# Transposing w3 on VectorE, from 32-row blocks, in place of TensorE

## Chip, core and metric

The kernel runs on one core of a Trainium2 chip. The metric is the device time of one execution in microseconds (us). The kernel before takes 873.46 us, the median of 3 runs (872.48 to 873.71). The profile shows one execution with a span of 870.7 us.

## What is computed

Eight batches of eight heads, 576 positions, 64 values per head. A retention (attention with a decay in place of a softmax) gives x, 4608 tokens by 512; a feed-forward block follows, in which two projections are multiplied element by element:

```python
scores = scale * np.matmul(q, k.transpose(0, 1, 3, 2))
ret = scores * Dmat[None, :, :, :]          # decay, zero above the diagonal
attn_out = np.matmul(ret, v)
x = attn_out.transpose(0, 2, 1, 3).reshape(B * S, H * D)   # 4608 x 512
a = x @ w1                                  # w1, w2: 512 x 1024
b = x @ w2
h = a * b @ w3                              # w3: 1024 x 1024
out = (h @ w_out).astype(np.float32)        # w_out: 1024 x 512
```

Queries, keys and values arrive as 32-bit floats; the four weights arrive as 64-bit floats, and the kernel converts them itself.

## The kernel before

The kernel doesn't compute h. It multiplies the two weights first, w3 @ w_out (1024 x 512, called w3o), once, and then a * b by w3o. This document is about that product of weights, a stage between the first feed-forward projections and the second half of the attention. TensorE takes its stationary operand transposed, so each block row of w3 (128 rows of 1024) has to be turned before it can be multiplied by w_out.

The weights are cut in blocks of 512 KB, 128 partitions by 512 numbers of 64 bits: 16 blocks for w1 and w2, 8 of w_out (`wo`), 16 of w3 (two for each block row). `load_block` fetches a block into one of five buffers:

```python
    blocks = []
    for fp in range(NQ):
        for j, w in enumerate((moe_w1, moe_w2)):
            for r in range(2):
                blocks.append((("w12", fp, j, r), w))
    blocks += [(("wo", g), moe_w_out) for g in range(KF)]
    blocks += [(("w3", ft, g0), moe_w3) for ft in range(KF) for g0 in range(0, DF, CV)]
    at = {key: n for n, (key, _) in enumerate(blocks)}
    loaded, begun, converted, turned = [0], [0], [0], [0]
...
    def load_block():
        n = loaded[0]
        if n == len(blocks):
            return
        key, w = blocks[n]
        t = raw.tile([P, CV, 2], I32, tag="raw", name="raw", bufs=5)
        if key[0] == "w12":
...
        else:
            r, c0 = (key[1], 0) if key[0] == "wo" else key[1:]
            nc.sync.dma_start(t, w[r * P:(r + 1) * P, c0:c0 + CV, :])
        live["raw", n] = t
        loaded[0] += 1
```

A block is converted by integer arithmetic on its two 32-bit halves: five instructions on VectorE and, between the third and the fourth, two on ScalarE. It is written as a generator, so that its steps can be laid between other work; `convert(n)` takes n steps.

```python
    def begin_block():
        n = begun[0]
        t = live["raw", n]
        lo, hi = t[:, :, 0], t[:, :, 1]
        e = raw.tile([P, CV], I32, tag="exp", name="e")
        m = raw.tile([P, CV], I32, tag="man", name="m")
        vec = nc.vector


        vec.tensor_scalar(out=e, in0=hi, scalar1=1, scalar2=21,
                          op0=ALU.logical_shift_left, op1=ALU.logical_shift_right)
        yield

        vec.tensor_scalar(out=m, in0=hi, scalar1=0x000FFFFF, scalar2=0x00100000,
                          op0=ALU.bitwise_and, op1=ALU.bitwise_or)
        yield
        vec.scalar_tensor_tensor(m.bitcast(F32), in0=lo.bitcast(U32), scalar=2.0 ** -32, in1=m,
                                 op0=ALU.mult, op1=ALU.add)
        relu = mybir.ActivationFunctionType.Relu
        nc.scalar.activation(e, e, relu, bias=lim[:, 0:1], scale=-1.0)
        nc.scalar.activation(e, e, relu, bias=lim[:, 1:2], scale=-2.0 ** 23)
        live["em", n] = e, m
        begun[0] += 1
        yield

    def end_block():
        n = converted[0]
        hi = live["raw", n][:, :, 1]
        e, m = live["em", n]
        vec = nc.vector
        vec.scalar_tensor_tensor(e, in0=hi, scalar=-(1 << 31), in1=e,
                                 op0=ALU.bitwise_and, op1=ALU.bitwise_or)
        yield
        key = blocks[n][0]
        while not (key[0] == "w12" or "wo" in live and (key[0] == "wo" or key[1] < turned[0] + 2)):
            yield "wait"
        out, m, e = converted_to(n), m.bitcast(F32), e.bitcast(F32)
        if key[0] == "w12":
            m, e = (x.rearrange("p (c n) -> p c n", c=2) for x in (m, e))
        vec.scalar_tensor_tensor(out, in0=m, scalar=2.0 ** -20, in1=e, op0=ALU.mult, op1=ALU.mult)
        converted[0] += 1

        if n >= 4:
            load_block()
        if key[0] == "w12" and key[1] > 0 and key[2:] == (1, 1):
            yield from strassen_weights(key[1])
        yield
```

In the conversion of a run of blocks, the beginning of the next block stands before the end of the present one:

```python
        yield from begin_block()
        while converted[0] < len(blocks):
            if begun[0] < len(blocks) and converted[0] not in (1, 2, 3):
                yield from begin_block()
            yield from end_block()
            if begun[0] == converted[0] < len(blocks):
                yield from begin_block()

```

The turning on TensorE and the product:

```python
    def w3_tr(ft):
        t = pools["wst"].tile([P, KF, P], F32, tag="w3T", name="w3T")
        for i in range(0, KF, NP):
            tp = acc.tile([P, NP, P], F32, tag="acc", name="tp")
            for n in range(NP):
                nc.tensor.transpose(tp[:, n, :], live["w3", ft][:, (i + n) * P:(i + n + 1) * P],
                                    ident)
            nc.scalar.copy(t[:, i:i + NP, :], tp)
        live["w3T", ft] = t

    def w3_mm(ft, part):
        if part == 0:
            live["w3ps"] = acc.tile([P, DM], F32, tag="acc", name="ps")
        ps = live["w3ps"]
        for g in range(part * NP, part * NP + NP):
            nc.tensor.matmul(ps, live["w3T", ft][:, g, :], live["wo"][:, g, :],
                             start=(g == 0), stop=(g == KF - 1))
        if part == 1:
            nc.scalar.copy(live["w3o"][:, ft, :], ps)
```

The up-projections (`up`) run on TensorE during the conversion; their additions on VectorE carry steps of the conversion between them:

```python
        def plus(ps, to, sb):
            nc.vector.tensor_add(c[:, to], ps, c[:, sb])
            convert(conv)
            if aside:
                aside.pop(0)()
...
        c = ffn.tile([P, 4, 2, TB], F32, tag="c", name="c", bufs=1)
        p1 = product(None, "A11", "B11")
        nc.scalar.copy(c[:, 0], p1)
        plus(product(None, "S2", "T2"), 1, 0)
        plus(product(None, "S3", "T3"), 2, 1)
        p5 = product(None, "S1", "T1")
        plus(p5, 3, 2)
        plus(product(None, "A22", "-T4"), 2, 2)
        product(p1, "A12", "B21")
        nc.scalar.copy(c[:, 0], p1)
        product(p5, "S4", "B22")
        plus(p5, 1, 1)
...
        nc.vector.tensor_mul(ab[:, 4 * fp:4 * fp + 4, :], c[:, :, 0, :], c[:, :, 1, :])
        if tail:
            convert(conv)
```

The loop of the stage. `todo` holds the up-projections left; when it is empty, the block rows follow each other:

```python
    live["wo"] = pools["wst"].tile([P, KF, DM], F32, tag="wo", name="wo", bufs=1)
    live["w3o"] = w3op.tile([P, KF, DM], F32, tag="w3o", name="w3o")
    todo = [(0, 1, 2), (0, 0, 3), (0, 1, 3)] + [(0, 2, fp) for fp in range(NQ - 1)]
    multiplied = 0
    while multiplied < KF:
        if todo:
            first = converted[0] < 4 * NQ
            up(*todo.pop(0), conv=2 if first else 1)
            convert(0 if first else 3)
        ft = multiplied
        begun_ft = ft < turned[0]
        if begun_ft:
            w3_mm(ft, 0)
        if turned[0] < KF and (not todo or converted[0] > at["w3", turned[0], DF - CV]):
            convert_up_to(at["w3", turned[0], DF - CV] + 1)
            w3_tr(turned[0])
            turned[0] += 1
        if begun_ft:
            w3_mm(ft, 1)
            multiplied += 1
        if not todo:
            convert(10)
    w3_part.close()
```

After it come the last up-projection of this token group, the down-projection by w3o, and the loads of the next heads (`ld_k`, `ld_q`, `ld_v`), which take the place in memory that the raw weight blocks had. Heads later in the kernel are already turned by VectorE (`front_blocks`, L198), from blocks of 32 rows, which the change now does for w3.

Of the kernel before, what the change touches and what calls it, by code (L numbers as in the profile page):

```python
# [8 lines left out]
F32 = mybir.dt.float32  # L9
I32 = mybir.dt.int32  # L10
U32 = mybir.dt.uint32
ALU = mybir.AluOpType
PSUM = bass.MemoryType.PSUM

# [22 lines left out]
def kernel(  # L39
# [13 lines left out]
    nc = tc.nc  # L53
    moe_w1, moe_w2, moe_w3, moe_w_out = (
        w.bitcast(I32).rearrange("r (c t) -> r c t", t=2) for w in (moe_w1, moe_w2, moe_w3, moe_w_out))
    B, H, S, D = q.shape
    DM = H * D
    DF = moe_w3.shape[0]
    CV = 512
    P = 128  # L60
    NP = H // 2
    NB2 = B // 2


    NC = (S + P - 1) // P
    short = S - (NC - 1) * P
    sizes = [short] + [P] * (NC - 1)
    starts = [0] + [short + c * P for c in range(NC - 1)]
    G = NB2 * NC
    NB = 3  # L70
    TB = S // NB
    NT = 2 * TB // P
    KD = DM // P
    KF = DF // P
# [13 lines left out]
    pools = {}  # L88
# [6 lines left out]
    open_attention(att_part)  # L95
    acc = ctx.enter_context(tc.tile_pool(name="acc", bufs=7, space=PSUM))
    st_ps = ctx.enter_context(tc.tile_pool(name="st_ps", bufs=1, space=PSUM))

    ctx.enter_context(tc.manual_schedule())

    live = {}
# [14 lines left out]
    ident = const.tile([P, P], F32, tag="ident", name="ident")  # L116
# [10 lines left out]
    gq = const.tile([P, NC, H], F32, tag="gq", name="gq")  # L127
    gqs = const.tile([P, NP, S // 32], F32, tag="gqs", name="gqs")
    dq = ffn.tile([P, 4, 2, TB], F32, tag="c", name="dq", bufs=1).rearrange("p a b s -> p (a b s)")[:H, :S]
# [6 lines left out]
    for c in (0, slice(1, NC)):  # L136
        n = short if c == 0 else P
# [16 lines left out]
    def strassen_weights(fp):  # L154
# [7 lines left out]
        tt("S4", "A12", "S2", ALU.subtract)  # L162
        live["S", fp] = True
        yield

    BL = 32

    def load_blocks(g, nm):

        i, c = divmod(g, NC)  # L170
        n = sizes[c] // BL
        t = pools["ld"].tile([P, 2 * NP, P // BL, BL], F32, tag="ld_q", name="bl_" + nm)
        src = {"k": k, "q": q}[nm][2 * i:2 * i + 2].rearrange("b (p a) s d -> a (b p) s d", a=2)
        for a in range(2):
            for f in range(D // BL):
                part = (a * (D // BL) + f) * BL
                for m in range(n):
                    s0 = starts[c] + m * BL
                    nc.sync.dma_start(t[part:part + BL, :, m, :],
                                      src[a, :, s0:s0 + BL, f * BL:(f + 1) * BL].rearrange("m r x -> r m x"))  # L180
        live["bl_" + nm, g] = t

    def scale_blocks(g):
# [3 lines left out]
        for b in range(2):  # L187
            part = t[:, b * NP:(b + 1) * NP, :n, :]
            nc.gpsimd.tensor_tensor(
                out=part, in0=part, in1=gqs[:, :, n0:n0 + n].unsqueeze(3).to_broadcast([P, NP, n, BL]),  # L190
                op=ALU.mult)

    def front_blocks(g):
        c = g % NC
        n = sizes[c] // BL
        for nm in "kq":
            dst = pools["fr"].tile([P, 2, NP, P], F32, tag=nm + "T", name=nm + "T", bufs=1 if nm == "k" else 2)
            nc.vector.transpose(  # L198
# [16 lines left out]
    def front(g, names="kq"):  # L215
        c = g % NC
        sz = sizes[c]
        for nm in names:
            src = live[nm, g]
            dst = pools["fr"].tile([P, 2, NP, P], F32, tag=nm + "T", name=nm + "T",  # L220
                                   bufs=1 if nm == "k" and g >= NC else 2)
# [87 lines left out]
    blocks = []  # L309
# [2 lines left out]
            for r in range(2):  # L312
                blocks.append((("w12", fp, j, r), w))
    blocks += [(("wo", g), moe_w_out) for g in range(KF)]
    blocks += [(("w3", ft, g0), moe_w3) for ft in range(KF) for g0 in range(0, DF, CV)]
    at = {key: n for n, (key, _) in enumerate(blocks)}
    loaded, begun, converted, turned = [0], [0], [0], [0]

    def load_block():
        n = loaded[0]  # L320
# [5 lines that stand above are left out]
            _, fp, _, r = key  # L326
            src = w[2 * r * P:2 * (r + 1) * P, fp * QC:(fp + 1) * QC, :]
            t2 = t.rearrange("p (c n) t -> p c n t", c=2)
            if r == 0:
                nc.sync.dma_start(t2, src.rearrange("(c p) n t -> p c n t", p=P))  # L330
            else:
                for half in range(2):
                    nc.sync.dma_start(t2[heads[half]],
                                      src.rearrange("(c a d) n t -> a d c n t", a=2, d=D)[1 - half])
        else:
            r, c0 = (key[1], 0) if key[0] == "wo" else key[1:]
            nc.sync.dma_start(t, w[r * P:(r + 1) * P, c0:c0 + CV, :])
        live["raw", n] = t
        loaded[0] += 1

    def converted_to(n):
        key, _ = blocks[n]
        if key[0] == "w12":
            _, fp, j, r = key
            return wA[fp // 2][:, j, 2 * r:2 * r + 2, fp % 2 * QC:fp % 2 * QC + QC]
        if key[0] == "wo":
            return live["wo"][:, key[1], :]
        _, ft, g0 = key
        if ("w3", ft) not in live:
            live["w3", ft] = pools["wst"].tile([P, DF], F32, tag="w3", name="w3")  # L350
        return live["w3", ft][:, g0:g0 + CV]

    def begin_block():
        n = begun[0]
# [23 lines left out]
# [6 lines that stand above are left out]
                                 op0=ALU.bitwise_and, op1=ALU.bitwise_or)  # L384
        yield
        key = blocks[n][0]
        while not (key[0] == "w12" or "wo" in live and (key[0] == "wo" or key[1] < turned[0] + 2)):
            yield "wait"
        out, m, e = converted_to(n), m.bitcast(F32), e.bitcast(F32)
        if key[0] == "w12":  # L390
            m, e = (x.rearrange("p (c n) -> p c n", c=2) for x in (m, e))
        vec.scalar_tensor_tensor(out, in0=m, scalar=2.0 ** -20, in1=e, op0=ALU.mult, op1=ALU.mult)  # L392
        converted[0] += 1

        if n >= 4:
# [4 lines that stand above are left out]
# [22 lines left out]
    def convert(n):  # L422

        for _ in range(n):
            if go_on() is not None:
                return

    def convert_up_to(n):
        while converted[0] < n:
            assert go_on() is None  # L430


    def w3_tr(ft):
        t = pools["wst"].tile([P, KF, P], F32, tag="w3T", name="w3T")
        for i in range(0, KF, NP):
            tp = acc.tile([P, NP, P], F32, tag="acc", name="tp")
            for n in range(NP):
                nc.tensor.transpose(tp[:, n, :], live["w3", ft][:, (i + n) * P:(i + n + 1) * P],  # L438
                                    ident)
            nc.scalar.copy(t[:, i:i + NP, :], tp)  # L440
        live["w3T", ft] = t

    def w3_mm(ft, part):
        if part == 0:
            live["w3ps"] = acc.tile([P, DM], F32, tag="acc", name="ps")
        ps = live["w3ps"]
        for g in range(part * NP, part * NP + NP):
            nc.tensor.matmul(ps, live["w3T", ft][:, g, :], live["wo"][:, g, :],  # L448
                             start=(g == 0), stop=(g == KF - 1))
        if part == 1:  # L450
            nc.scalar.copy(live["w3o"][:, ft, :], ps)

    every = [(i, n) for i in range(NB2) for n in range(NB)]

# [190 lines left out]


    load_block()
    load(0, "v")
    load_block()
    load(1, "kq")  # L650
    load_block()
# [65 lines left out]
    for a in range(2):  # L717
        for f in range(D // BL):
            part = (a * (D // BL) + f) * BL
# [6 lines left out]
    live["wo"] = pools["wst"].tile([P, KF, DM], F32, tag="wo", name="wo", bufs=1)  # L726
    live["w3o"] = w3op.tile([P, KF, DM], F32, tag="w3o", name="w3o")
    todo = [(0, 1, 2), (0, 0, 3), (0, 1, 3)] + [(0, 2, fp) for fp in range(NQ - 1)]
    multiplied = 0
    while multiplied < KF:  # L730
        if todo:
            first = converted[0] < 4 * NQ
            up(*todo.pop(0), conv=2 if first else 1)
            convert(0 if first else 3)
        ft = multiplied
        begun_ft = ft < turned[0]
        if begun_ft:
            w3_mm(ft, 0)
        if turned[0] < KF and (not todo or converted[0] > at["w3", turned[0], DF - CV]):
            convert_up_to(at["w3", turned[0], DF - CV] + 1)  # L740
            w3_tr(turned[0])
            turned[0] += 1
        if begun_ft:
            w3_mm(ft, 1)
            multiplied += 1
        if not todo:
            convert(10)
    w3_part.close()


# [15 lines left out]
    todo = [(down, (0, 0), (0, 1)), (down, (1, 0), (1, 1)), (down, (0, 2), (1, 2))]  # L766
# [38 lines left out]
    for g in range(NC, G):  # L805
        c = g % NC
        n = -(-len(todo) // (NC - c))
# [78 lines left out]
```

## Time and profile before

| what | value |
|---|---|
| time, median of 3 runs | 873.46 us |
| span of the profiled execution | 870.7 us |
| TensorE (PE) busy in it | 851.9 us |
| VectorE (DVE) busy | 458.3 us |
| ScalarE (ACT) busy | 194.7 us |
| GpSimd (POOL) busy | 111.8 us |
| first transpose of w3 on TensorE | 158.79 us from the start |
| first matmul after the stage | 222.57 us from the start |

How the lines are read: a group has its source line, engine, operation, the tile written and the tiles read, the shape and the count; after the first bar the busy time of all in us and the mean length of one in ns; after the second the time for which the engine stood idle just before them, with what ended most of it. "PEld" is the loading of TensorE's weights, beside its matmuls. The chain of waits is followed back from the last instruction: at each step to what released it, or to the instruction before it on its engine. In a timeline each row has its start and its length in us; a bracket at the end gives the idle time before it, and the releaser. "issue" is time in which an engine waited for nothing that the profile shows.

### The profile page before, as it was taken

The page shows a single profiled execution, that of the slowest core. Times are in us where ns is not written, and L with a number is a line of the kernel's source. Part 1 is how long each engine was busy: PE and PEld are TensorE (multiplying, and loading weights), DVE is VectorE, ACT ScalarE, POOL GpSimd, SP SyncE. Part 2 cuts the span into 40 slices and gives each one's busy share as a digit, 9 for nine tenths or more (in the row PEclk, how much of TensorE's full clock was granted, in tenths as well). Part 3 has the DMA queues.
Part 4 walks back from the last instruction along what each step waited for, and adds up shares of the span by engine and source line. Part 5 has one row for each costly group of instructions (what it writes and reads, how often), then busy time and mean ns, then how long its engine had stood idle before and what let it go on. Part 6 is the DMA issues. An engine that isn't in the chain of part 4 may idle for free.

```text
span 870.7 us, 15305 instructions
## 1 busy us (share of the span) xinstructions
PE 851.9 (98%) x6373; PEld 779.0 (89%) x6373; DVE 458.3 (53%) x781; ACT 194.7 (22%) x390; POOL 111.8 (13%) x91
## 2 busy tenths in 40 slices
PE   5899999999999999999999999999999999999998
PEld 5899999645888999999999999999999999999996
DVE  4799998973543344643544544534543434334343
ACT  3676333553022221101111101111101100001000
POOL 3000020002001323201212030230300101000000
PEclk9999999999999999999999999999999999999999
DMA  9993443437035444515242335061300000000001
GB/s 194 218 223 107 98 99 104 139 120 108 1 77 118 114 63 82 95 28 93 49 84 44 55 68 96 27 104 34 59 25 25 2 25 1 25 24 1 25 1 49
DMA packets 187332, 63.20 MB, mean 73 GB/s; under 512 B 175480, under 2 KB 175480, under 8 KB 187264
## 3 DMA queue, kind: packets, MB, share of 16 engines
q1 hardware_dynamic: 154624, 54.07, 29.2%
q10 hardware_dynamic: 32640, 8.16, 4.9%
q8 instruction: 50, 0.82, 0.4%
q14 instruction: 18, 0.15, 0.1%
HBM read 52.76 MB, written 9.44 MB: 71 GB/s over the span
## 4 chain that ended last, share of the span: by engine, by line
PE 88%; DVE 3%; issue 1%; DMA 1%; ACT 1%; DVEq 0%; ACTq 0%; SPq 0%
PE up L493 46%; PE po L599 25%; PE ps L448 6%; PE sc L241 4%; PE xps L298 3%; PE xps L291 2%; PE tp L226 1%; PE st L263 1%; DVE c L498 1%; PE tp L438 1%; DVE e L383 0%; DMA raw<-in_moe_w_dram 0%; ACT e L372 0%; DVE ab L519 0%; DVE w L392 0%
## 5 line engine op out<-in xcount | busy, mean ns | idle before, releaser
L498 DVE TENSOR_TENSOR c<-up,c 128x384 f32<-128x384 f32 x240 | 133.2, 555 | 198.0 <-PE up L493 193.2
L493 PE MATMUL up<-xT,wA 128*128 128x192 f32 x1152 | 213.5, 329 | 1.0 <-ACT xT L303 1.0
L493 PEld LDWEIGHTS up<-xT,wA 128*128 128x128 f32 x1152 | 191.9, 191 | 3.6 <-ACT xT L303 1.2
L493 PE MATMUL up<-T,wS 128*128 128x192 f32 x768 | 141.1, 327 | 2.1 <-DVE T L467 2.1
L493 PEld LDWEIGHTS up<-T,wS 128*128 128x128 f32 x768 | 127.8, 191 | 2.4 <-issue 2.4
L599 PE MATMUL po<-w3o,ab 128*128 128x256 f32 x456 | 104.2, 381 | 0.3 <-ACT ot L621 0.3
L599 PEld LDWEIGHTS po<-w3o,ab 128*128 128x128 f32 x456 | 86.0, 190 | 12.1 <-ACT ot L621 0.7
L603 DVE TENSOR_TENSOR ot<-po,ot 128x256 f32<-128x256 f32 x90 | 38.1, 424 | 72.3 <-PE po L599 70.6
L513 ACT COPY c<-up 128x384 f32<-128x384 f32 x48 | 22.9, 477 | 226.3 <-PE up L493 222.0
L493 PE MATMUL up<-xT,wS 128*128 128x192 f32 x384 | 70.6, 327 | 0.6 <-DVE c L498 0.5
L493 PE MATMUL up<-T,wA 128*128 128x192 f32 x384 | 70.3, 326 | 0.0
L244 DVE TENSOR_TENSOR pm<-sc,mask 128x512 f32<-128x512 f32 (+1 forms) x80 | 45.5, 628 | 46.7 <-PE sc L241 46.5
L599 PE MATMUL po<-wB,forms 128*128 128x256 f32 x288 | 65.1, 379 | 0.0
L493 PEld LDWEIGHTS up<-xT,wS 128*128 128x128 f32 x384 | 63.6, 190 | 1.5 <-DVE c L498 1.5
L493 PEld LDWEIGHTS up<-T,wA 128*128 128x128 f32 x384 | 63.7, 190 | 0.0
L599 PEld LDWEIGHTS po<-wB,forms 128*128 128x128 f32 x288 | 54.8, 190 | 7.3
L212 POOL TENSOR_TENSOR ld_v<-ld_v,gk 128x1024 f32<-128x1024 f32 (+1 forms) x17 | 32.3, 1900 | 213.6 <-DMA ld_v<-in_v_dram 186.3
L448 PE MATMUL ps<-wo,w3T 128*128 128x512 f32 x128 | 56.4, 593 | 0.2 <-ACT w3T L440 0.2
L506 ACT COPY c<-up 128x384 f32<-128x384 f32 x48 | 22.8, 476 | 117.4 <-PE up L493 68.4
L467 POOL TENSOR_TENSOR T<-xT,T 128x384 f32<-128x384 f32 x20 | 20.9, 1043 | 217.1 <-PE up L493 215.4
L519 DVE TENSOR_TENSOR ab<-c 128x768 f32<-128x768 f32 x48 | 46.6, 972 | 3.8
L448 PEld LDWEIGHTS ps<-wo,w3T 128*128 128x128 f32 x128 | 23.7, 190 | 27.2 <-issue 26.7
(75 smaller groups left out, 817.8 us busy)
## 6 DMA issues: line engine op xcount, KB each, us to landing
raw<-in_moe_w_dram SPq DMA_DIRECT2D x24, 512.0 KB, 3.7
out_dram<-ot SPq DMA_DIRECT2D x24, 256.0 KB, 2.0
bl_q<-in_q_dram SPq DMA_DIRECT2D x136, 32.0 KB, 2.1
bl_k<-in_k_dram SPq DMA_DIRECT2D x136, 32.0 KB, 2.2
raw<-in_moe_w_dram SPq DMA_DIRECT2D x16, 256.0 KB, 6.1
ld_k<-in_k_dram SPq DMA_DIRECT2D x8, 512.0 KB, 7.1
ld_q<-in_q_dram SPq DMA_DIRECT2D x8, 512.0 KB, 8.2
ld_v<-in_v_dram SPq DMA_DIRECT2D x8, 512.0 KB, 7.4
```

What stands on the lines that cost most here:

```text
L212: nc.gpsimd.tensor_tensor(out=t, in0=t, in1=gam[:sz, c].unsqueeze(1).unsqueeze(3).to_broadcast([sz, 2, H, D]), op=ALU.mult)
L241: nc.tensor.matmul(sc[j][:sz, p, :sz], kT[hs, b, p, :sz], qT[hs, b, p, :sz], start=True, stop=True)
L244: nc.vector.tensor_mul(pm[:sz, b, j, :, :sz], sc[j][:sz, :, :sz], mask[:sz, :sz].unsqueeze(1).to_broadcast([sz, NP, sz]))
L298: nc.tensor.matmul(banks[r][heads[half], b, n, :sz], vs[:sz, b * H + 2 * p + j, :], pm[:sz, b, j, p, :sz], start=(c == 0 and m == 0), stop ...
L448: nc.tensor.matmul(ps, live["w3T", ft][:, g, :], live["wo"][:, g, :], start=(g == 0), stop=(g == KF - 1))
L493: nc.tensor.matmul(ps[:, w, :], a[:, w, r, :], b[:, r, :], start=(new and w == r == 0), stop=(w == r == 1), skip_group_check=True)
L498: nc.vector.tensor_add(c[:, to], ps, c[:, sb])
L506: nc.scalar.copy(c[:, 0], p1)
L513: nc.scalar.copy(c[:, 0], p1)
L519: nc.vector.tensor_mul(ab[:, 4 * fp:4 * fp + 4, :], c[:, :, 0, :], c[:, :, 1, :])
L599: nc.tensor.matmul(ps[nm], a[A][:, f, :], live["W"][B][:, f, :], start=(f == 0 and not on), stop=(f == NP - 1), skip_group_check=True)
L603: nc.vector.tensor_add(ot[:, to[0], to[1]], ps[nm], ot[:, sb[0], sb[1]])
```

## The change

w3 is loaded in another layout and turned by VectorE in place of TensorE. VectorE's transpose turns each 32 x 32 square within its own 32 partitions. So the four quarters of a block row's columns are put on the four groups of 32 partitions, each with its rows in four blocks of 32; a transpose of 128 x 1024 then gives the whole block row turned, in SBUF, with the 1024 columns of w3 in another order on partitions. The rows of w_out are loaded in the same other order, so that the product is the same. What it is for: TensorE is left to multiply, and ScalarE need not copy turned blocks out of PSUM. The conversion's arithmetic stays as it was.

The diff, cut to its core (declarations moved, blank lines and the renaming of a counter left out):

```diff
 load_block:
-        else:
-            r, c0 = (key[1], 0) if key[0] == "wo" else key[1:]
-            nc.sync.dma_start(t, w[r * P:(r + 1) * P, c0:c0 + CV, :])
+        elif key[0] == "wo":
+            nc.sync.dma_start(t, w.rearrange("(a i x) n t -> i a x n t", i=KF, x=BL)[key[1]])
+        else:
+            _, ft, h = key
+            src = w[ft * P:(ft + 1) * P].rearrange("(j r) (a h f) t -> h a r j f t", r=BL, a=QP, h=DF // CV)
+            for a in range(QP):
+                nc.sync.dma_start(t[a * BL:(a + 1) * BL].rearrange("p (j f) t -> p j f t", j=P // BL), src[h, a])
 converted_to:
-        if ("w3", ft) not in live:
-            live["w3", ft] = pools["wst"].tile([P, DF], F32, tag="w3", name="w3")
-        return live["w3", ft][:, g0:g0 + CV]
+        if h == 0:
+            live["w3"] = pools["wst"].tile([P, P // BL, DF // CV, CV // QP], F32, tag="w3", name="w3", bufs=1)
+        return live["w3"][:, :, h, :]
 end_block:
-        while not (key[0] == "w12" or "wo" in live and (key[0] == "wo" or key[1] < turned[0] + 2)):
+        while not (key[0] == "w12" or "wo" in live and (key[0] == "wo" or key[1] < multiplied[0] + 3)):
             yield "wait"
         ...
         vec.scalar_tensor_tensor(out, in0=m, scalar=2.0 ** -20, in1=e, op0=ALU.mult, op1=ALU.mult)
+        if key[0] == "w3" and key[2] == DF // CV - 1:
+            yield
+            t = pools["wst"].tile([P, KF, P], F32, tag="w3T", name="w3T", bufs=3)
+            vec.transpose(t.rearrange("p i (j r) -> p j i r", r=BL),
+                          live["w3"].rearrange("p j h f -> p (j h f)"))
+            live["w3T", key[1]] = t
 the product:
-    def w3_tr(ft):
-        ...                                  # 8 transposes on TensorE, 2 copies on ScalarE
-    def w3_mm(ft, part):
-        ...                                  # half of the 8 matmuls at a time
+    def w3_mm(ft):
+        ps = acc.tile([P, DM], F32, tag="acc", name="ps")
+        for g in range(KF):
             nc.tensor.matmul(ps, live["w3T", ft][:, g, :], live["wo"][:, g, :],
                              start=(g == 0), stop=(g == KF - 1))
+        nc.scalar.copy(live["w3o"][:, ft, :], ps)
+        multiplied[0] += 1
 the loop:
+    while multiplied[0] < KF:
+        ft = multiplied[0]
+        done = at["w3", ft, DF // CV - 1] + 1
+        ready = converted[0] >= done
         if todo:
             first = converted[0] < 4 * NQ
             up(*todo.pop(0), conv=2 if first else 1)
             convert(0 if first else 3)
-        ...                                  # w3_mm half, w3_tr of the next, w3_mm half
+        if ready or not todo:
+            convert_up_to(done)
+            w3_mm(ft)
         if not todo:
-            convert(10)
+            convert(11)
```

In the program that results, the eight products stand in a row on TensorE, behind the same up-projection as the first transposes did before. On ScalarE the copy of each product (`w3o`) stands ahead of the activations of two blocks.

More of the change, by code (lines that the diff above doesn't have):

```diff
@@ L60 @@
     P = 128
+    BL = 32
+    QP = P // BL
     NP = H // 2
@@ L164, in strassen_weights @@
         yield
-    BL = 32
     def load_blocks(g, nm):
@@ L314 @@
     blocks += [(("wo", g), moe_w_out) for g in range(KF)]
-    blocks += [(("w3", ft, g0), moe_w3) for ft in range(KF) for g0 in range(0, DF, CV)]
+    blocks += [(("w3", ft, h), moe_w3) for ft in range(KF) for h in range(DF // CV)]
     at = {key: n for n, (key, _) in enumerate(blocks)}
-    loaded, begun, converted, turned = [0], [0], [0], [0]
+    loaded, begun, converted, multiplied = [0], [0], [0], [0]
     def load_block():
@@ L347, in converted_to @@
             return live["wo"][:, key[1], :]
-        _, ft, g0 = key
-        if ("w3", ft) not in live:
-            live["w3", ft] = pools["wst"].tile([P, DF], F32, tag="w3", name="w3")
-        return live["w3", ft][:, g0:g0 + CV]
+        _, ft, h = key
+        if h == 0:
+            live["w3"] = pools["wst"].tile([P, P // BL, DF // CV, CV // QP], F32, tag="w3", name="w3", bufs=1)
+        return live["w3"][:, :, h, :]
     def begin_block():
@@ L391, in end_block @@
             m, e = (x.rearrange("p (c n) -> p c n", c=2) for x in (m, e))
+        if key[0] == "w3":
+            m, e = (x.rearrange("p (c n) -> p c n", c=P // BL) for x in (m, e))
         vec.scalar_tensor_tensor(out, in0=m, scalar=2.0 ** -20, in1=e, op0=ALU.mult, op1=ALU.mult)
+        if key[0] == "w3" and key[2] == DF // CV - 1:
[4 more added lines that the diff above has]
+            live["w3T", key[1]] = t
         converted[0] += 1
@@ L430, in convert_up_to @@
             assert go_on() is None
-    def w3_tr(ft):
[L434 to L441, printed above, removed]
-    def w3_mm(ft, part):
[L444 to L447, printed above, removed]
+    def w3_mm(ft):
+        ps = acc.tile([P, DM], F32, tag="acc", name="ps")
+        for g in range(KF):
             nc.tensor.matmul(ps, live["w3T", ft][:, g, :], live["wo"][:, g, :],
                              start=(g == 0), stop=(g == KF - 1))
-        if part == 1:
-            nc.scalar.copy(live["w3o"][:, ft, :], ps)
+        nc.scalar.copy(live["w3o"][:, ft, :], ps)
+        multiplied[0] += 1
     every = [(i, n) for i in range(NB2) for n in range(NB)]
@@ L728 @@
     todo = [(0, 1, 2), (0, 0, 3), (0, 1, 3)] + [(0, 2, fp) for fp in range(NQ - 1)]
-    multiplied = 0
-    while multiplied < KF:
+    while multiplied[0] < KF:
+        ft = multiplied[0]
+        done = at["w3", ft, DF // CV - 1] + 1
+        ready = converted[0] >= done
         if todo:
@@ L734 @@
             convert(0 if first else 3)
[L735 to L745, printed above, removed]
+        if ready or not todo:
+            convert_up_to(done)
+            w3_mm(ft)
         if not todo:
-            convert(10)
+            convert(11)
     w3_part.close()
```

## The prediction

> **What bounds the kernel now.** I read the page first. Section 1 says which engine is full, section 2 whether it is full throughout and at what clock.
>
> ```profile
> PE 851.9 (98%) x6373; PEld 779.0 (89%) x6373; DVE 458.3 (53%) x781; ACT 194.7 (22%) x390; POOL 111.8 (13%) x91
> ...
> PEclk9999999999999999999999999999999999999999
> ```
>
> TensorE is busy 98% of the span at full clock, so a microsecond taken off TensorE is worth a microsecond unless another engine's wait takes its place. VectorE's 53% is an average over stages. The change touches only one stage, w3 @ w_out, so I look there next: the groups of instructions, shapes kept apart, for the lines of this stage (x128 stands for 64 matmuls of the program: an f32 matmul is recorded twice, a transpose once).
>
> ```profile
> L448 PE MATMUL ps<-wo,w3T 128*128 128x512 f32 x128 | 56.4, 593 | 0.2 <-ACT w3T L440 0.2
> L440 ACT COPY w3T<-tp 128x512 f32<-128x512 f32 x16 | 8.6, 587 | 5.9 <-PE tp L438 5.8
> L438 PE MATMUL tp<-ident,w 128*128 128x128 f32 x64 | 8.5, 273 | 1.1 <-DVE w L392 1.1
> L392 DVE SCALAR_TENSOR_TENSOR w<-m,e 128x512 f32<-128x512 f32 x16 | 11.1, 691 | 0.9
> L198 DVE STREAM_TRANSPOSE kT<-bl_k 128x1024 f32<-128x1024 f32 x8 | 9.9, 1239 | 0.0
> L198 DVE STREAM_TRANSPOSE qT<-bl_q 128x1024 f32<-128x1024 f32 x8 | 9.6, 1202 | 0.0
> ```
>
> 273 ns is the length of one transpose, not its price, since they overlap. The price comes from the chain of waits, in order of time, in this stage:
>
> ```profile
> 164.51 0.70 DVE w L392
> 165.21 0.14 issue
> 165.35 0.63 PE tp L438 x4
> 165.98 6.87 PE ps L448 x16
> 172.84 0.88 PE tp L438 x8
> 173.72 6.87 PE ps L448 x16
> ```
>
> From 165.35 on the chain stays on TensorE until the stage ends at 222.6 (the next stage's first matmul is there at 222.57). One block row of w3 costs 6.87 + 0.88 = 7.75 us: 8 matmuls at 0.86, 8 transposes at 0.11. VectorE keeps up with slack: the table by stage gives it 5.59 us of work in the 7.74 us from 180.43. Its timeline shows its waits, all on ScalarE:
>
> ```profile
> 184.35 0.69 DVE L369 SCALAR_TENSOR_TENSOR m<-raw,m 128x512 f32<-128x512 uint32 x1
> 186.92 0.69 DVE L383 SCALAR_TENSOR_TENSOR e<-raw,e 128x512 int32<-128x512 int32 x1 [1.88 <-ACT e L373]
> ```
>
> and ScalarE's timeline shows why: its queue is in order, and the copy of a finished product stands ahead of the two activations that VectorE waits for.
>
> ```profile
> 184.93 0.58 ACT L451 COPY w3o<-ps 128x512 f32<-128x512 f32 x1 [2.79 <-PE ps L448]
> 185.41 0.72 ACT L372 ACTIVATE e<-e,lim 128x512 int32<-128x512 int32 x1
> 186.17 0.72 ACT L373 ACTIVATE e<-e,lim 128x512 int32<-128x512 int32 x1
> ```
>
> So there is a loop TensorE, ScalarE, VectorE, TensorE already. It costs nothing now, because TensorE is always the last of it.
>
> [...]
>
> **The change part by part.**
>
> Removed, TensorE: 64 transposes, 8 x 0.88 = 7.0 us, all on the path, and the first wait for VectorE (1.14 us before 165.35) and for the first copy (0.24 at 160.07) in their present form. If nothing took their place, the stage would be 8 x 6.87 = 55.0 us from 158.8 to 213.8 in place of 222.6: at most 8.8 us, 1.0%, to be had.
>
> Removed, ScalarE: 16 copies of 587 ns, 1.07 us per block row. Off the path in steady state, but it shortens the loop.
>
> Added, VectorE: 8 transposes of 128x1024, 1.24 us each by the L198 rows (same size and type; only the output is written in blocks of 32 columns). They stand between w's second half and the next block's conversion.
>
> Moved: the loads of w3 become 64 DMAs of 128 KB in place of 16 of 512 KB. The DMA share in 168.5 to 188.4 is 0.46, five raw buffers run ahead, and VectorE's waits in this stage name no DMA. I count 0. The product is no longer cut in two around the next transposes: 8 matmuls in a row once the transposed block row is there. w3 has one buffer, w3T three, in place of two and two: the same room, and VectorE may still run ahead.
>
> Now the steady state, by engine and block row:
> - TensorE 6.87.
> - VectorE: the pitches of the timeline between starts (0.34, 0.45, 0.61, 0.76, 0.73 for the five conversions of one block) make 2.89, twice is 5.78, plus the transpose, 1.24 less the 0.08 by which such instructions overlap: about 7.0. So VectorE is now slightly slower than TensorE.
> - The loop. In the order of the changed program on ScalarE, each w3o copy stands ahead of two pairs of activations; the first pair belongs to the block row two further on. From the start of product k: 6.87 to its end, 0.04 + 0.48 for the copy, 1.51 for the pair, then on VectorE e 0.80, w 0.73, the begin of the next block 1.40, e 0.72, w 0.73, transpose 1.24, 0.05 to the start of product k+2. The sum is 14.57 for two block rows, 7.28 each. This is the longest of the three.
>
> The start: the first transpose falls into the last up-product, after the addition at 156.78, so it runs about 157.3 to 158.5, ready when TensorE has finished the up-product at 158.8: product 0 runs 158.8 to 165.7. VectorE's w of the next block row ended at 165.2 (164.51 + 0.70); one transpose ahead of it delays it by 1.16 and its own transpose ends at 167.6. So product 1 starts at 167.7, a wait of 2.0 us. From there: product 2 at 174.6 (VectorE), 3 at 182.3 (loop: 167.7 + 14.57), 4 at 189.3, 5 at 196.8, 6 at 203.9. For the last one no block is left to begin, which takes 1.40 off the loop: 196.8 + 13.2 = 210.0, but product 6 ends at 210.8, so product 7 runs 210.8 to 217.7. The stage ends 222.6 - 217.7 = **4.9 us** earlier, of the 8.8 at most. The rest is 2.0 at the start and some 1.9 in small waits of 0.1 to 0.8 us.
>
> After the stage: VectorE's last conversion ends about 4 us later than now (208.4 against 204.5 + 0.7), so the loads of the next heads, which wait for its buffers and start at 203.1 now, move to about 206.5. Their last scaling on GpSimd ends at 219.6 now, so at about 223; TensorE wants these heads at 243.9 - 4.9 = 239.0. Hidden by 16 us. The gain stays.
>
> Sum: 873.5 - 4.9 = **868.6 us**, 0.6% less.
>
> **The rivals.**
> - VectorE becomes the bound by more than I count. For it: 7.0 against 6.87 leaves no slack, and the transpose writes its output scattered in pieces of 128 B, which L198 doesn't quite do. [...] Each 0.1 us more on a transpose is 0.8 us in all; at 2 us a transpose the gain is gone (about 874), at 4 us it is some 890.
> - The loop doesn't bind, because the activations come sooner or waits overlap. Then 7.0 per block row, one microsecond or so better: 867.5. The floor, TensorE alone, is 873.5 - 8.8 = 864.7, only if the start had no wait either.
> - The loads become the bound: four issues per block on one queue, smaller pieces. For it: each piece is a quarter as long. Against: a block is needed every 3.5 us, one issue takes 0.33 us now, so four take about 1.3, and the DMA engines are half idle. If it did bind at 5 us a block, the stage would take 80 us, about 890.
> - The transposes were hidden anyway. Against: the chain lists them, each 0.88 us, in every block row. Then the time would stay at 873.
>
> **Range and chances.** The step I can misjudge is the wait per block row: 0.3 us either way on seven rows is about 2 us, and a slower transpose pulls only up. So 866.8 to 871.5 for 8 in 10. The ceiling of 1.0% rules out faster by over 2%; slower by over 2% (891) needs a transpose of 4 us or loads at 5 us a block.
>
> **What would show it.** Right: the 64 TensorE transposes and L440's copies gone; 8 VectorE transposes 128x1024 near 1.24 us; the product's matmuls still 64 at 6.87 us per eight; one wait near 2 us before product 1, then starts 6.9 to 7.7 us apart; the chain of waits in this stage alternating between TensorE, ScalarE's w3o copy and activations, and VectorE; the first matmul after it near 217.7; no DMA named in VectorE's waits. Wrong: transposes of 2 us or more, VectorE waiting for raw, or TensorE waiting for keys and queries near 240 us.

## The result, and the profile after

The changed kernel takes 877.02 us (median of 4 runs, 875.72 to 877.11); the kernel before, on the same chip, 873.10 (4 runs). The ratio is 1.0041, with a 95% interval of 1.0024 to 1.0059: the change costs 3.9 us where I had expected a gain of 4.9. The profiled spans are 875.0 and 870.7 us.

The page of the changed kernel, sections 1 and 2:

```profile
PE 848.9 (97%) x6309; PEld 773.9 (88%) x6309; DVE 469.8 (54%) x789; ACT 186.0 (21%) x374; POOL 113.5 (13%) x91
PEclk9999998999999999999999999999999999999999
```

The transposes are off TensorE: 64 instructions fewer than before. Yet it is busy only 3.0 us less (851.9 before), though 7.0 us of work were taken off. The one 8 in the row of its clock says where to look: the seventh slice is 131 to 153 us, ahead of the stage that the change is about.

The groups of the stage itself, shapes kept apart:

```profile
L450 PE MATMUL ps<-wo,w3T 128*128 128x512 f32 x128 | 56.1, 596 | 2.9 <-DVE w3T L404 2.9
L404 DVE STREAM_TRANSPOSE w3T<-w 128x1024 f32<-128x1024 f32 x8 | 9.9, 1244 | 0.6
```

The product is the same work as before (56.1 us against 56.4), its waits come to 2.9 us in all, and a transpose by VectorE takes 1244 ns. TensorE's timeline shows the stage from its first product to the first matmul of the next stage (start, length, and in brackets the idle time before it with its releaser):

```profile
166.37 7.03 PE L450 MATMUL ps<-wo,w3T 128*128 128x512 f32 x16
174.72 13.97 PE L450 MATMUL ps<-wo,w3T 128*128 128x512 f32 x32 [1.32 <-DVE w3T L404]
189.53 14.10 PE L450 MATMUL ps<-wo,w3T 128*128 128x512 f32 x32 [0.84 <-DVE w3T L404]
204.37 20.97 PE L450 MATMUL ps<-wo,w3T 128*128 128x512 f32 x48 [0.74 <-DVE w3T L404]
225.17 1.46 PE L495 MATMUL up<-xT,wA 128*128 128x192 f32 x8
```

From 166.37 to 225.17 are 58.80 us. Before, the same stretch (first transpose at 158.79 to 222.57) was 63.78. **The stage is 4.98 us shorter, as predicted (4.9), but it begins 7.6 us later.** The loss lies before it. Going back in the same timeline, I found the place:

```profile
129.69 1.46 PE L495 MATMUL up<-xT,wA 128*128 128x192 f32 x8
134.63 2.93 PE L495 MATMUL up<-xT,wS 128*128 128x192 f32 x8 [3.48 <-DVE c L500]
137.35 2.77 PE L495 MATMUL up<-xT,wA 128*128 128x192 f32 x8
139.91 1.67 PE L495 MATMUL up<-T,wS 128*128 128x192 f32 x8
```

TensorE stands idle for 3.48 us, waiting for an addition by VectorE, and then two groups of 8 matmuls take 2.93 and 2.77 us in place of 1.46. VectorE's timeline says why it was late, and the table by stage (stretch, its length, busy time of TensorE, its weight loads, VectorE, ScalarE and GpSimd, then granted clock, share of the DMA engines, GB/s) what the matmuls ran at:

```profile
131.81 0.43 DVE L368 TENSOR_SCALAR e<-raw 128x512 int32<-128x512 int32 x1 [4.41 <-DMA raw<-in_moe_w_out_dram]
```

```profile
134.60:138.00 3.40, 3.37 (x11) 3.37 (x12) 2.04 (x4) 0.00 (x0) 0.00 (x0) 0.50 0.45 147
```

VectorE waited for a block of **w_out**, which the prediction never looked at. Set against the profile of a repaired version (e1 below), the same instruction is later in the changed kernel by 1.1 us at 67 us, by 4.75 where TensorE resumes after the idle time (129.9 against 134.6), by 7.43 when the two slow groups are done (132.5 against 139.9), and by 8.4 at the end. So the parts of the loss are 1.1 in the first 67 us, 3.6 of idle time, 2.7 of half clock and 0.95 after it. Of this last, 0.74 is one wait of TensorE for ScalarE near the end (1.04 us at 862.47, 0.30 in e1); e2 below, with w_out loaded in the same way, has 0.31 there, so this part isn't w_out's.

Why was the block late? The diff also reorders the loading of w_out: its rows must stand in the order in which the new transpose leaves the columns of w3. In the stretch from 95 to 103 us only w_out is being loaded. The table by stage for it, first for the kernel before, then for the changed one:

```profile
95.00:103.00 8.00, 8.00 (x52) 8.00 (x51) 7.89 (x16) 3.73 (x6) 0.00 (x0) 1.00 0.37 128
```

```profile
95.00:103.00 8.00, 8.00 (x51) 8.00 (x50) 7.90 (x15) 3.49 (x6) 0.00 (x0) 1.00 0.25 100
```

The last two columns: share of 16 engines, and GB/s. A steady share of 0.25 is that of 4 engines of 16, busy all the time. A block is 128 packets of 4 KB (one row of w_out, 512 values x 8 B); a packet takes about 162 ns in the changed kernel and 160 before (medians). By these numbers a block takes an estimated 32 x 162 ns = 5.2 us on 4 engines, and 512 KB at 100 GB/s come to the same. Before, a block landed 3.5 us after its issue (the median). The view of the queue that issues the loads (SP), first for the kernel before, then the changed one, shows what this meets:

```profile
102.54 10.51 SPq L721 DMA_DIRECT2D gqs<-decay_q_dram  x16
113.15 7.43 SPq L337 DMA_DIRECT2D raw<-in_moe_w_out_dram  x3
```

```profile
103.78 17.70 SPq L723 DMA_DIRECT2D gqs<-decay_q_dram  x16
121.57 1.82 SPq L338 DMA_DIRECT2D raw<-in_moe_w_out_dram  x3
```

In the middle of the w_out blocks stand 16 small loads of a decay table (`gqs`, in pieces of 4 B), on the same queue. One of them held the queue for 7.33 us in the changed kernel (the longest before: 1.78). The last three w_out blocks were therefore issued from 121.57 on instead of from 113.15, close upon each other, at 5.2 us apiece.

### The profile page after: what moved, and what is told of

It reads as the page before. It is cut to its first block, busy times and chain, and to the rows that moved or that the text cites. A ratio compares the mean times of both kernels' runs of the same rounds, so it can differ in the third digit from the quotient of the medians.

```text
span 875.0 us, 15231 instructions
## 1 busy us (share of the span) xinstructions
PE 848.9 (97%) x6309; PEld 773.9 (88%) x6309; DVE 469.8 (54%) x789; ACT 186.0 (21%) x374; POOL 113.5 (13%) x91
## 4 chain that ended last, share of the span: by engine, by line
PE 85%; DVE 8%; DMA 3%; issue 2%; ACT 1%; POOL 0%; DVEq 0%; SPq 0%; ACTq 0%; POOLq 0%
PE up L495 45%; PE po L601 24%; PE ps L450 4%; PE sc L243 4%; PE xps L300 3%; PE tp L228 2%; DVE c L500 2%; PE xps L293 2%; PE st L265 1%; DMA raw<-in_moe_w_out_dram 1%; DMA ld_q<-in_q_dram 1%; DVE e L389 1%; DMA ld_k<-in_k_dram 1%; DVE w L400 1%; DVE pm L246 1%
## 5 line engine op out<-in xcount | busy, mean ns | idle before, releaser
L450 PE MATMUL ps<-wo,w3T 128*128 128x512 f32 x128 | 56.1, 596 | 2.9 <-DVE w3T L404 2.9
```

## The experiments

Two theories stood at first. **A:** the reordered load of w_out is the cause, since its outermost dimension has 4 steps and so only 4 engines carry it, and the small loads behind it hold the queue. **B:** it lies with the new stage: its loads of w3 or its other order on VectorE shift the start and throw things out of step.

**e1: the changed kernel, w_out's block in four transfers of 32 rows.** The order of the rows stays; each transfer now has its 32 rows outermost.

```diff
-            nc.sync.dma_start(t, w.rearrange("(a i x) n t -> i a x n t", i=KF, x=BL)[key[1]])
+            src = w.rearrange("(a i x) n t -> i a x n t", i=KF, x=BL)[key[1]]
+            for a in range(QP):
+                nc.sync.dma_start(t[a * BL:(a + 1) * BL], src[a])
```

> The changed kernel, with each block of w_out loaded by four transfers of 32 rows each in place of one transfer over four groups of rows. Theory A (the one-transfer form of the reordered w_out load runs on 4 of the 16 DMA engines, 5.2 us a block, arrives late, and VectorE, then TensorE, wait for it at 127 to 135 us): the packets of w_out run at a DMA share near 1 again, VectorE's wait of 4.4 us for w_out is gone, TensorE's clock stays full near 135 us, and the time falls by the 3.5 us of idle and some 2.9 us at lower clock, from 877.0 to about 870.6. Rival B (the w3 loads in smaller pieces, or the order of rows itself, is what is slow): no change, 877.

Measured: 868.58 us (868.46 to 869.74), ratio to the kernel before 0.9953 (0.9939 to 0.9967). The table by stage and TensorE's timeline of e1:

```profile
95.00:103.00 8.00, 8.00 (x51) 8.00 (x50) 7.89 (x15) 3.73 (x6) 0.00 (x0) 1.00 0.42 121
```

```profile
158.72 7.03 PE L452 MATMUL ps<-wo,w3T 128*128 128x512 f32 x16
167.06 13.97 PE L452 MATMUL ps<-wo,w3T 128*128 128x512 f32 x32 [1.31 <-DVE w3T L406]
181.87 14.10 PE L452 MATMUL ps<-wo,w3T 128*128 128x512 f32 x32 [0.84 <-DVE w3T L406]
196.71 20.97 PE L452 MATMUL ps<-wo,w3T 128*128 128x512 f32 x48 [0.74 <-DVE w3T L406]
217.52 1.46 PE L497 MATMUL up<-xT,wA 128*128 128x192 f32 x8
```

The share is 0.42 in place of 0.25 (0.37 in the kernel before; I had expected near 1), the 3.48 us of idle time and the clock of 0.50 are gone (1.00 from 134.6 to 138 us), and the stage runs from 158.72 to 217.52, again 58.80 us long. By the two profiles the kernel is 8.4 us shorter (875.0 to 866.6), and 6.5 of these lie where w_out made VectorE late; the rest is the 1.1 in the first 67 us and the 0.74 near the end. Theory B falls as the main cause: all of the new stage is in e1.

**e2: the kernel before, with w_out alone loaded as in the change.** It pairs columns of w3 with other rows of w_out, so it computes another product; the work and the times of instructions are those of the kernel before.

```diff
+        elif key[0] == "wo":
+            nc.sync.dma_start(t, w.rearrange("(a i x) n t -> i a x n t", i=KF, x=32)[key[1]])
         else:
-            r, c0 = (key[1], 0) if key[0] == "wo" else key[1:]
+            r, c0 = key[1:]
```

> The kernel before, with one part of the change alone: w_out is loaded in the changed kernel's order of rows, by one transfer a block. w3 is loaded and turned as before, so the sum pairs columns of w3 with other rows of w_out; the amount of work is the same. Theory A: the w_out blocks come late here as well, with a DMA share near 0.25 while they run; VectorE waits 4 to 5 us for w_out near 127 us, and the time rises by about 6.4 us to 879.5. Rival B (it is the w3 loads, or VectorE's transposes): 873, as before.

Measured: 880.37 us (879.03 to 880.91), ratio 1.0082 (1.0065 to 1.0099): the load alone costs 6.9 us. The same two lines as in the changed kernel appear, VectorE's and TensorE's timeline of e2:

```profile
133.00 0.43 DVE L364 TENSOR_SCALAR e<-raw 128x512 int32<-128x512 int32 x1 [5.45 <-DMA raw<-in_moe_w_out_dram]
```

```profile
135.81 2.20 PE L495 MATMUL up<-xT,wS 128*128 128x192 f32 x8 [4.52 <-DVE c L500]
```

So the cause is shown from both sides: put alone into the old kernel it brings the loss, taken out of the new one it removes it. By size they agree too: e2's profile is 7.7 us longer than that of the kernel before, 1.1 of it in the first 67 us, which leaves 6.6 put in, against 6.5 taken out.

**e3 and e4: the small loads later.** e3 is the changed kernel, w_out in one transfer still, with the 16 `gqs` loads behind the stage; e4 the kernel before with the same move, as the control.

```diff
 (the loop of 16, moved from before the stage ...)
-            nc.sync.dma_start(gqs[part:part + BL, p, :], decay_q[2 * p + a]...)
 w3_part.close()
 (... to here)
+            nc.sync.dma_start(gqs[part:part + BL, p, :], decay_q[2 * p + a]...)
```

> The changed kernel, with w_out as it is there (one transfer a block), but the 16 small loads of the decay table (pieces of 4 bytes) moved from the middle of the w_out loads to the end of the stage. Theory A, in its narrow form (a slow w_out load hurts only because the small loads back up behind it on the same queue and hold up the last three w_out loads by 8 us): VectorE's wait for w_out is gone or under 1 us, about 870.6. Rival: 5.2 us a block is too slow by itself, the wait stays, 876 to 877.

> The kernel before with the same 16 small loads moved to the end of the stage: the control for the run before this one. In the kernel before no w_out block comes late, so 873.1 within 0.7 us by every theory; if it is faster by 2 us or more, moving them has a value of its own and the run before this one can't be read as I mean to.

Measured: e3 869.13 us (867.51 to 870.84), ratio 0.9958 (0.9942 to 0.9974); e4 873.58, ratio 1.000 (0.999 to 1.001). In e3's view of the queue, all eight w_out blocks are issued in one row, each as a buffer comes free:

```profile
81.00 39.28 SPq L338 DMA_DIRECT2D raw<-in_moe_w_out_dram  x8
```

and VectorE's waits name w_out no more. So here a share of 0.26 (from 95 to 103 us), some 4 engines of 16, was enough for w_out once the small loads were out of the way: eight issues in 39 us are some 5.6 us apart, a little more than the estimated 5.2 us that a block takes on 4 engines. It takes both, the narrow transfer and the small loads behind it, to make the loss; the move alone (e4) is worth nothing. What exactly holds one small load for 7.33 us inside the queue, the trace does not show. Pieces of 4 B are not what it takes: in the changed kernel one issue of w3's loads, in pieces of 1 KB, was held for 4.66 us behind the last w_out blocks (0.44 at most in e1), and in e8 below issues of w_out itself for up to 5.67.

**e5: e1, with ScalarE's copy of a finished product behind the next pair of activations.** It tests the rival of the prediction in which VectorE rather than the loop sets the pace.

```diff
-            nc.scalar.copy(live["w3o"][:, ft, :], ps)
+            live["w3ps", ft] = ps
 ...
         (after the steps of the conversion)
+        if multiplied[0] > ft:
+            nc.scalar.copy(live["w3o"][:, ft, :], live["w3ps", ft])
```

> The changed kernel with w_out in four transfers a block (the first of these runs, 868.6), and ScalarE's copy of each product moved behind the next two pairs of activations in its queue. Loop theory (the copy, which waits for the product, holds up the activations, these the conversion, and so every second product, by 0.84 and 0.74 us): VectorE's waits for ScalarE in the stage (4.2 us in all) go, products start 6.9 to 7.0 us apart, and the stage ends about 1.5 us sooner: 867.1. Rival (VectorE's own work, 7.0 us a block row, is the bound): the waits go, but product starts stay as far apart on average, 868.4 or so.

Measured: 866.68 us (865.68 to 867.87), ratio 0.9926 (0.9912 to 0.9939); e1 was 0.9953 in another session. TensorE's timeline of e5:

```profile
158.80 7.03 PE L452 MATMUL ps<-wo,w3T 128*128 128x512 f32 x16
167.13 48.39 PE L452 MATMUL ps<-wo,w3T 128*128 128x512 f32 x112 [1.31 <-DVE w3T L406]
215.35 1.46 PE L497 MATMUL up<-xT,wA 128*128 128x192 f32 x8
```

After product 1 starts, the other products follow without a wait: seven in 48.39 us, 6.9 each. So the loop over ScalarE's queue was what bound the stage, and VectorE by itself keeps up with TensorE. The stage ends 2.2 us sooner than in e1.

**e6: e1, with the scaling of one block of values (`ld_v`) on ScalarE instead of GpSimd.** In the changed kernel, after the stage, one of VectorE's sums of w3o takes twice as long as the others. VectorE's and GpSimd's timeline of the changed kernel:

```profile
230.12 2.46 DVE L538 TENSOR_TENSOR wB<-w3o 128x1024 f32<-128x1024 f32 x1
232.97 1.21 DVE L538 TENSOR_TENSOR wB<-w3o,wB 128x1024 f32<-128x1024 f32 x1
```

```profile
228.87 2.63 POOL L214 TENSOR_TENSOR ld_v<-ld_v,gk 128x1024 f32<-128x1024 f32 x1 [0.27 <-DMA ld_v<-in_v_dram]
```

GpSimd's instruction overlaps the sum before (from 228.52, 1.22 us long) and this one; in the kernel before, where it meets neither, it takes 1.90 us. It ends at 231.50, and VectorE's sum 1.08 us later. The edit:

```diff
-        scale(g + 1, "v")
+        scale(g + 1, "v", g == NC)
```

> The changed kernel with w_out in four transfers a block, and the scaling of one block of values, which in the changed kernel falls on GpSimd beside VectorE's sums of w3o (2.62 us there in place of 1.90, while VectorE's sum takes 2.45 in place of 1.21), done on ScalarE instead. Theory: the two slow each other, so the sum is back at 1.21 us, TensorE's wait of 0.5 us before the down-projection is gone, and the time falls by about 1.0 us, to 867.6. Rival: VectorE's slow sum has another cause (its operands' place, a semaphore), stays at 2.45 and the time at 868.6.

Measured: 867.20 us (867.1 to 868.65), ratio 0.9935 (0.9922 to 0.9947). In e6's timeline the sum is back at its length:

```profile
223.46 1.21 DVE L540 TENSOR_TENSOR wB<-w3o 128x1024 f32<-128x1024 f32 x1
```

and TensorE's wait of 0.5 us that followed it is gone. So it was the scaling on GpSimd beside it that made the sum longer, 2.46 us in place of 1.21; why it did, the trace does not show. The time saved, about one microsecond by the trace, is within what the intervals of e1 and e6 leave open. (The profiled spans are equal, 866.6 us, but e6's execution carries 1.05 us of a wait in the first 67 us that e1's lacks.)

**e7: e1, e3's move, e5 and e6 together.**

> All together: w_out in four transfers a block, the small loads of the decay table after the stage, the copies behind the activations, the value block scaled on ScalarE. If the two gains add, 868.6 - 1.5 - 1.0 = 866.1; if VectorE's own rate is the bound of the stage, 867.4.

Measured: 866.84 us (864.48 to 867.09), ratio 0.9923 (0.991 to 0.9936). That can't be told apart from e5 alone (0.9926). In the times the gains of the parts don't add. In the profiles they do: e7's execution has the early wait (1.28 us behind e5 at 58 us) and ends 0.37 us behind, so 0.9 came back after the stage, where the scaling was moved.

**e8: the changed kernel, w_out's block in two transfers of two groups of 32 rows.** This is a harder test of theory A: each transfer now has 2 steps outermost.

```diff
+            for a in range(0, QP, 2):
+                nc.sync.dma_start(t[a * BL:(a + 2) * BL], src[a:a + 2])
```

> The changed kernel with each block of w_out in two transfers of two groups of 32 rows each. Theory A in its exact form (a transfer's packets spread over as many DMA engines as its outermost dimension has steps, here 2): each transfer still has 64 packets of 162 ns on 2 engines, 5.2 us, two at a time, a DMA share of 0.25 while they run, and the time stays at 876 to 877. Rival (more transfers in flight is what helped in the first run): share and rate double, and the time falls to 869 to 871.

Measured: 914.62 us (913.57 to 915.89), ratio 1.0475 (1.0459 to 1.0491). Table by stage, and from the lists of waits of VectorE and TensorE (total us, times, longest):

```profile
95.00:103.00 8.00, 8.00 (x52) 8.00 (x51) 7.90 (x16) 3.73 (x6) 0.00 (x0) 1.00 0.13 52
```

```profile
DVE e L370 <- DMA raw<-in_moe_w_out_dram: 42.3, 6, 16.2
```

```profile
PE up L497 <- DVE c L502: 35.0, 4, 17.9
```

The share is 0.13, that of 2 engines of 16, and the rate halves from 100 to 52 GB/s: an estimated 64 x 162 ns = 10.4 us a block. In these two forms the share went with the number of outermost steps of one transfer, as A has it (0.25 with 4, 0.13 with 2), but no figure for the time that was written before the run held. The packet records say the same: of the time in which w_out is moving, two packets are in flight for 94% in e8 and four for 83% in the changed kernel; in the kernel before it is most often 16 (for 33%). So the second transfer did not add to the share; the trace doesn't number the engines, and which ones carried the two transfers was not shown. With 32 outermost steps (e1) the share was 0.42 and the rate 121 GB/s, and the four transfers helped; with 2 the two transfers harmed.

## Why the prediction was wrong, point by point

**The step that failed is "Moved: the loads of w3 ... I count 0".** It priced w3's loads, and rightly: no wait on them costs anything. But it left out the other load that the diff rewrites, w_out's, and that term is 6.5 us. VectorE waits 4.41 us for a block of w_out, and TensorE, which waits for VectorE's addition, stands idle for 3.48 us and then runs at a clock of 0.50. At a share of 0.25 a block took an estimated 5.2 us, the small loads backed up behind it on the queue, and the last three blocks were issued from 121.57 us on in place of 113.15. The shift between e1 and the changed kernel is 8.4, but 1.1 of it lies in the first 67 us, ahead of any w_out block, and 0.74 near the end. The 1.1 does not need the change: a wait of 1.2 to 1.3 us on w1/w2's weights early on is in the profiles of the changed kernel, e2, e4, e6 and e7 and not in those of the kernel before, e1, e3 and e5, and e4's program differs from the kernel before only after 100 us, e6's from e1 only after the stage. The cause of the 0.74 stays open. The 3.6 us of idle time and the 2.7 of half clock are settled.

The loads' rival ("The loads become the bound") had the right kind of cause and the wrong load: it asked for the size of pieces and the number of issues, and the block of w_out has large pieces (4 KB) and one issue. What counted was over how many engines one transfer was spread: the share was 0.25 with one transfer of 4 outermost steps, 0.13 with e8's two of 2, and 0.42 with e1's four of 32. The working had not asked for that.

The sum without that term stands: e1 is the kernel that the prediction described, and takes 868.58 us where it said 868.6. Step by step, against e1:
- **Removed and added.** 64 transposes and 16 copies gone; 8 transposes on VectorE at 1244 ns (1.24 predicted). Writing in pieces of 128 B costs nothing to be seen beside the 1239 and 1202 ns of L198's two before. The rival that the transposes were hidden anyway falls too, for the stage is 4.98 us shorter.
- **The start.** Product 0 at 158.72 (158.8), product 1 at 167.06 (167.7): a wait of 1.31, not 2.0 us.
- **The pace.** Products at 181.87 and 196.71 for numbers 3 and 5 (182.3, 196.8), the next stage at 217.52 (217.7). The loop of 14.57 us measures 14.81 and 14.84 by these starts. In e1's chain of waits it stands as drawn: product 1 to 174.18, ScalarE's copy and pair of activations to 176.17, VectorE to 181.83, product 3 at 181.87. Product 1 came 0.6 us sooner and two rounds of the loop took 0.5 longer, so these two errors cancel in the end of the stage. VectorE's own pace was put a little too high: transposes without a wait between them start 6.83 to 6.97 us apart, where the sum said 7.0. So it keeps pace with TensorE, and e5 shows what this leaves to be had, 2.2 us. The rival "the loop doesn't bind" (867.5) is what e5 made, with 866.68.
- **After the stage: "Hidden by 16 us".** TensorE indeed didn't wait for the heads. VectorE's last conversion ended at 208.66 (208.4 in the sum), 3.4 us later than before, where the prediction's words say about 4. But the later loads moved GpSimd's scaling onto VectorE's sums of w3o, and between the kernel before and e1 a gain of 5.0 us shrinks to 4.0 there. That step looked at who waits for the loads and not at what else runs when they land. Side by side, VectorE's sum took 2.46 us in place of 1.21 and GpSimd's scaling 2.63 in place of 1.90. e1's agreement to the tenth is thus partly luck: by the two profiled executions its gain is 4.0 us, by the medians 4.9, and the interval of its ratio allows 2.9 to 5.3.

Of the signs named, "VectorE waiting for raw" was on the list of what would show it wrong, and it is what the trace showed, for a tensor that the working had not priced.

## What to carry to other kernels

For every transfer that a diff touches, also those that only follow suit, read the outermost dimension of its access pattern: put the 32 or 128 partitions there, and where a reordering puts a short one there, cut the transfer along it (here a share of 0.42 with 32 steps outermost and 0.37 with 128, against 0.25 with 4; 868.58 us in place of 877.02). Then ask what stands behind it on the same queue. When work moves between engines by a few microseconds, look at what its loads and its followers now run beside (here a sum of 2.46 us in place of 1.21); and when an in-order queue serves two partners, put what the slower one waits for first (here the activations ahead of the copy, 2.2 us).

The change with w_out in four transfers and the copy behind the activations (e5) takes 0.9926 of the time before; of the versions measured only e7, which can't be told apart from it, is as fast.

## What the runs showed of the hardware that I had not expected

- One transfer with 4 outermost steps had a share of 0.25 of the DMA engines: 100 GB/s, an estimated 5.2 us for 512 KB (32 packets of 162 ns on each of 4 engines). With 2 steps, two transfers together had a share of 0.13: 52 GB/s and, by the same working, 10.4 us. The bytes and the pieces of 4 KB were the same.
- One load in pieces of 4 B held the issuing queue for 7.33 us behind such transfers (7.34 in e2, 10.70 in e8), and for 1.78 at most in the kernel before.
- After 3.48 us of idle time TensorE's first two groups of matmuls ran at a granted clock of 0.50 (from 133.5 to 140.3 us in the changed kernel, 1.00 from 140.4 on), which cost 2.7 us more, three quarters of the wait itself. The cost did not grow with the wait: after 4.52 us of idle time in e2 it was 1.8 us.
